# Four key heads per load on 32 partitions each, with block transposes of the weights, in a cached-attention decode kernel

## The chip, the cores and the metric

The kernel runs on one core of one Trainium2 chip. The metric is the device time of one execution in microseconds (us).

## The reference, cut to what matters

For 8 batch rows with one token each, the reference computes a gated sum of an attention over a key/value cache and a small MLP.

```python
W = min(4096, max(256, Sk // 4))          # 1024: only the last 1024 of 4096 cached keys count
q = (x @ wq)                              # 16 query heads of 256, 2 for each of 8 key heads
k = jnp.repeat(k_cache[:, :, Sk - W:, :], rep, axis=1)
v = jnp.repeat(v_cache[:, :, Sk - W:, :], rep, axis=1)
p = softmax(einsum("bhqd,bhkd->bhqk", q, k) * Dh ** -0.5)
a = einsum("bhqk,bhkd->bhqd", p, v) ... @ wo
b = gelu(layernorm(x) @ w1 + b1) @ w2 + b2
return g * a + (1 - g) * b                # g = sigmoid(sum(x * gate_w))
```

All data is bf16. The keys and values that count are 8 x 8 x 1024 x 256 elements each, 67.1 MB together. The four weight matrices add 10.5 MB. Each key and value byte is used for two query heads only, so there is little arithmetic for each byte.

With these inputs the attention adds only a very small part to the output: with the values set to zero, the reference's output of rms 0.025 changes by an rms of 0.00004. The comparison with the reference therefore passes even when keys and values lie in the wrong order.

## The kernel before: the parts that matter

The work goes in 16 units. A unit is one batch row and four key heads, 2 MB of keys and 2 MB of values. Each 1 MB load holds two heads, interleaved over the partitions, and each partition receives one run of 8 KB:

```python
def kv_loader(src, b, g):                      # GP = 2 heads, NCK = 16 keys in a run
    def load(t):
        nc.sync.dma_start(
            t[:],                              # 128 partitions: p = 2 * s + head
            src[b, g : g + GP, kv_base:Sk, :].rearrange("a (s c) d -> s a (c d)", c=NCK),
        )
```

The loads go to a ring of 18 slots of 1 MB. The compute of a unit turns the keys on TensorE (PE), copies them out on VectorE (DVE) and ScalarE (ACT), makes the scores, and turns the exponentials with 16 small matmuls. The values are the stationary operand:

```python
def values(u, ET, rb):
    ...
            for j in range(NJ):
                for c in range(NCK):
                    o = c * Dh + j
                    nc.tensor.matmul(PO[:, j, cols],
                        lhsT=vn[:, o : (c + 1) * Dh : NJ],       # 128 x 128 values as weights
                        rhs=ET[:, c, cols], start=(c == 0), stop=(c == NCK - 1))
...
for u in range(1, NQ - 2):
    transpose_keys(u)
    values(u - 1, *weights(u - 1))
    scores(u)
    softmax(u)
```

Of the kernel before, what the change touches and what calls it, by code (L numbers as in the profile page):

```python
# [17 lines left out]
def kernel(  # L18
# [38 lines left out]
    GP = 2  # L57
    NCK = NC * GP
    SK = P // GP
    SLOT = 4096  # L60
# [4 lines left out]
    RING = 18  # L65
    NMM = 512
    CMM = NMM // SK
# [30 lines left out]
    def kv_loader(src, b, g):  # L98
        def load(t):
            nc.sync.dma_start(  # L100
                t[:],
                src[b, g : g + GP, kv_base:Sk, :].rearrange(
                    "a (s c) d -> s a (c d)", c=NCK
                ),
            )

        return load
# [22 lines left out]
    def add_kv(name, src, u):  # L130
        b, half = divmod(u, Hkv // QUAD)
        for s in range(2):
            add((name, u, s), kv_loader(src, b, half * QUAD + 2 * s))

    wq_m = A_wq[0:DM, :].rearrange("(p r) n -> p r n", r=NR)
# [5 lines left out]
    W2A = SLOT // D  # L141

    add_kv("k", A_k_cache, 0)
    add(("w1", 0), rows_loader([w1_m[:, 0 : 2 * F]]))
    add(("w1", 1), rows_loader([w1_m[:, 2 * F : 3 * F], w1_t]))
    for r in range(NR):
        add(("wq", r), rows_loader([wq_m[:, r, :]]))
    add(("wq", NR), rows_loader([wq_t]))
    add(("w2", 0), rows_loader([w2_v[:, 0 : W2A * D]]))
    add(("w2", 1), rows_loader([w2_v[:, W2A * D : NF * D]]))  # L150
# [7 lines left out]
    for q in range(NHQ):  # L158
        for j0, j1 in WO_PARTS[q]:
            add(("wo", q, j0), rows_loader([wo_v[:, q, j0 * D : j1 * D]]))  # L160

    def slot(*key):
        return slots[index[key]]
# [19 lines left out]
    nc.vector.memset(S_ps[:], 0.0)  # L183

# [15 lines left out]
    sel = consts.tile([P, RQ], BF16)  # L200
    qw = consts.tile([P, NJ, NB, Hq], BF16)
# [18 lines left out]
    for h in range(2):  # L220
        nc.vector.tensor_copy(xz[:, h, h::2], x_sb[:, DM:D])
    transposed(xT, x_sb, xz)
    nc.vector.tensor_copy(
        sel[:].rearrange("p (a i) -> p a i", i=rep),
        ident[:].rearrange("p (a s) -> p a s", a=QUAD)[:, :, 0:rep],
    )

    par = consts.tile([P, GP], F32)
    own = consts.tile([P, RQ], F32)
    nc.vector.reduce_sum(  # L230
        par[:], ident[:].rearrange("p (s a) -> p a s", a=GP), axis=AXIS.X
    )
    nc.vector.tensor_copy(
        own[:].rearrange("p (t a i) -> p t a i", a=GP, i=rep),
        par[:]
        .rearrange("p (t a i) -> p t a i", t=1, i=1)
        .to_broadcast([P, QUAD // GP, GP, rep]),
    )
# [61 lines left out]
    def transpose_keys(u):  # L300
        for s in range(2):
            kn = slot("k", u, s)
            kt = ktpool.tile([P, NJ, NCK, SK, GP], BF16, tag="kt", name="kt")
            KT[s] = kt
            ktf = kt[:].rearrange("p j c s a -> p j (c s a)")
            for c0 in range(0, NCK, NC):
                for j in range(NJ):
                    ktp = ps_kt.tile([P, W], BF16, tag="ktp", name="ktp")
                    for c in range(NC):
                        o = (c0 + c) * Dh + j * P  # L310
                        nc.tensor.transpose(  # L311
                            ktp[:, c * P : (c + 1) * P], kn[:, o : o + P], ident[:]
                        )
                    dst = ktf[:, j, c0 * P : (c0 + NC) * P]
                    if evac[0] % 8 in (2, 4, 7):
                        nc.scalar.copy(dst, ktp[:])  # L316
                    else:
                        nc.vector.tensor_copy(dst, ktp[:])  # L318
                    evac[0] += 1
            done()  # L320

    def query():
        qt = ps_misc.tile([P, Hq * NJ, NB], F32, tag="misc", name="qt")
        for r in range(NR + 1):
            w = slot("wq", r)
            for k in range(Hq * NJ):
# [4 lines left out]
                    lhsT=w[:, c : c + P],  # L331
# [5 lines left out]
            done()  # L337
        for j in range(NJ):
            nc.vector.tensor_scalar_mul(  # L339
                qw[:, j, :, :],  # L340
                qt[:].rearrange("p (h j) b -> p j b h", j=NJ)[:, j],
                qscale,
            )

    def scores(u):
        b, half = divmod(u, Hkv // QUAD)
        for hf in range(W // NMM):
            for j in range(NJ):
                for a in range(QUAD):
                    h0 = (half * QUAD + a) * rep  # L350
                    nc.tensor.matmul(  # L351
                        S_ps[32 * a : 32 * a + rep, hf * NMM : (hf + 1) * NMM],
                        lhsT=qw[:, j, b, h0 : h0 + rep],
                        rhs=KT[a // GP][:, j, hf * CMM : (hf + 1) * CMM, :, a % GP],
# [6 lines left out]
    def softmax(u):  # L361
        nmx = epool.tile([P, 1], F32, tag="nmx", name="nmx")
        nc.vector.reduce_max(nmx[:], S_ps[:], axis=AXIS.X, negate=True)  # L363
        E = epool.tile([P, W * GP], BF16, tag="E", name="E")
        rowsum = epool.tile([P, 1], F32, tag="rowsum", name="rowsum")
        nc.scalar.activation(  # L366
            E[:].rearrange("p (k a) -> p k a", a=GP),
            S_ps[:].rearrange("p (k o) -> p k o", o=1).to_broadcast([P, W, GP]),
            ACT.Exp,
            bias=nmx[:],  # L370
            scale=1.0,
            accum_out=rowsum[:],
# [3 lines left out]
    def weights(u):  # L376
        E, rowsum = soft.pop(u)
        rsum = epool.tile([P, 1], F32, tag="rsum", name="rsum")
        nc.vector.reciprocal(rsum[:], rowsum[:])
        selr = epool.tile([P, RQ], F32, tag="selr", name="selr")  # L380
        nc.vector.tensor_scalar(  # L381
            selr[:], sel[:], rsum[:], float(GP), op0=ALU.mult, op1=ALU.mult
        )
        sm = ps_sm.tile([P, NCK + 1, RQ], F32, tag="sm", name="sm")
# [208 lines left out]
```

## Time and profile before

| | before |
|---|---|
| time, median of 3 runs | 198.85 us (198.73 to 199.01) |
| span of the profiled run | 197.0 us |
| DMA queue of SyncE, share of 16 engines' span | 95.8% |
| rate in the middle of the run | 406 to 427 GB/s |
| one 8 KB packet (trace's DMA records, mean) | 317 ns |
| one 4 KB packet | 162 ns |
| loop of one unit in the chain of waits | 10.15 us |

From the two packet sizes, 4,096 B more cost 155 ns, which is 26.4 GB/s for one of the 16 DMA engines, and about 7 ns per packet are left over. Sixteen engines at 26.4 GB/s would make 422 GB/s.

The page of the kernel before: the busy tenths of the DMA engines and the rate in 40 equal slices of the span, and the queue that carries the loads.

```profile
DMA  4999999999999999999999999999999999999960
GB/s 170 416 427 406 420 412 414 421 414 424 411 414 419 419 419 416 414 419 419 423 411 411 423 416 423 409 418 423 416 416 413 418 419 419 421 411 416 413 246 23
...
q1 hardware_dynamic: 11424, 77.68, 95.8%
```

The DMA engines are busy to 9 tenths or more in every slice from the second to the 38th, at an even rate. This stream is the first limit. The costliest groups of compute come next, as line, engine, operation, output and inputs, then busy time and mean time of one instruction, then the idle time before them:

```profile
L311 PE MATMUL ktp<-ident,slot 128*128 128x128 bf16 x1024 | 73.9, 232 | 21.6 <-ACT kt L316 15.2
...
L366 ACT ACTIVATE E<-S_ps,nmx 128x2048 bf16<-128x2048 f32 x16 | 31.5, 1968 | 72.2 <-DVE nmx L363 72.2
...
L414 PE MATMUL po<-ET,slot 128*128 128x4 bf16 x1024 | 28.1, 164 | 5.3 <-DVE ET L395 5.3
...
L351 PE MATMUL S_ps<-kt,qw 128*2 128x512 bf16 x256 | 18.1, 402 | 0.4 <-DVE qw L339 0.4
```

The end of the chain of waits, in order of time (start, duration, what):

```profile
118.22 19.89 DMA slot<-in_A_v_cache_dram
...
138.17 21.37 DMA slot<-in_A_v_cache_dram
...
159.60 19.96 DMA slot<-in_A_v_cache_dram
...
179.62 13.82 DMA slot<-in_A_wo_dram
...
193.48 0.39 PE A_ps L545 x6
...
193.89 0.34 DVE res L552
```

From 118 us to 193.4 us the chain consists of loads alone, each one released by the load eight places ahead of it. Before 118 us it runs through compute, in a loop of 10.15 us for a unit. So compute keeps up with the stream, but has almost no slack. With the DMA engines busy throughout, a faster compute alone should gain little here.

### The profile page before, as it was taken

To read this page: it belongs to the slowest core of one execution; us is meant where nothing else is said; L and a number is where in the kernel's file an instruction comes from. 1 tells how busy PE (TensorE), PEld (TensorE's weight loads), DVE (VectorE), ACT (ScalarE), POOL (GpSimd) and SP (SyncE) were. 2 spreads that over 40 slices of the span, in tenths; PEclk is the share of its full clock that TensorE was granted. 3 is DMA by queue.
4 is the path that set the end of the run, shared out by engine and by line. 5 is a ranking of instruction groups with operands and counts; after the bars stand their busy time and mean duration, and the time that the engine had idled before them with its cause. 6 is when DMAs were issued, how large, how long until landed. Compare 5 with 4: busy or idle time off the path is not lost.

```text
span 197.0 us, 6578 instructions
## 1 busy us (share of the span) xinstructions
PE 147.7 (75%) x3006; PEld 125.1 (64%) x3006; DVE 94.3 (48%) x230; ACT 82.0 (42%) x85; POOL 0.9 (0%) x7
## 2 busy tenths in 40 slices
PE   1699869868686878979596868686868686887662
PEld 0699739656574758877575667575656665675641
DVE  6540335364646464555545454636363636763200
ACT  3250043272636354362718180808172727383000
POOL 1000000000000000000000000000000000000000
PEclk9996556999999996799999999999999999997555
DMA  4999999999999999999999999999999999999960
GB/s 170 416 427 406 420 412 414 421 414 424 411 414 419 419 419 416 414 419 419 423 411 411 423 416 423 409 418 423 416 416 413 418 419 419 421 411 416 413 246 23
DMA packets 11645, 78.10 MB, mean 396 GB/s; under 512 B 1489, under 2 KB 1890, under 8 KB 3042
## 3 DMA queue, kind: packets, MB, share of 16 engines
q1 hardware_dynamic: 11424, 77.68, 95.8%
q8 instruction: 23, 0.38, 0.8%
q10 hardware_dynamic: 194, 0.02, 0.1%
q14 instruction: 4, 0.03, 0.0%
HBM read 77.68 MB, written 0.01 MB: 394 GB/s over the span
## 4 chain that ended last, share of the span: by engine, by line
DMA 49%; PE 26%; DVE 16%; ACT 5%; issue 2%; SPq 0%; ACTq 0%
DMA slot<-in_A_v_cache_dram 31%; PE ktp L311 10%; DMA slot<-in_A_wq_dram 8%; DVE kt L318 7%; PE po L414 7%; DMA slot<-in_A_wo_dram 7%; DVE nmx L363 6%; PE S_ps L351 5%; ACT kt L316 4%; DMA slot<-in_A_k_cache_dram 3%; PE sm L393 2%; ACT E L366 1%; DVE ET L395 1%; DVE selr L381 1%; PE bb L484 1%
## 5 line engine op out<-in xcount | busy, mean ns | idle before, releaser
L311 PE MATMUL ktp<-ident,slot 128*128 128x128 bf16 x1024 | 73.9, 232 | 21.6 <-ACT kt L316 15.2
L311 PEld LDWEIGHTS <-slot 128*128 128x128 bf16 x1024 | 66.1, 105 | 33.3 <-issue 28.3
L318 DVE COPY kt<-ktp 128x1024 bf16<-128x1024 bf16 x80 | 52.5, 686 | 30.3 <-PE ktp L311 29.0
L366 ACT ACTIVATE E<-S_ps,nmx 128x2048 bf16<-128x2048 f32 x16 | 31.5, 1968 | 72.2 <-DVE nmx L363 72.2
L316 ACT COPY kt<-ktp 128x1024 bf16<-128x1024 bf16 x48 | 47.1, 1013 | 19.3 <-PE ktp L311 19.3
L414 PEld LDWEIGHTS <-slot 128*128 128x128 bf16 x1024 | 29.5, 99 | 6.8 <-issue 6.8
L414 PE MATMUL po<-ET,slot 128*128 128x4 bf16 x1024 | 28.1, 164 | 5.3 <-DVE ET L395 5.3
L363 DVE TENSOR_REDUCE nmx<-S_ps 128x1 f32<-128x1024 f32 x16 | 19.6, 1225 | 13.0 <-PE S_ps L351 13.0
L351 PE MATMUL S_ps<-kt,qw 128*2 128x512 bf16 x256 | 18.1, 402 | 0.4 <-DVE qw L339 0.4
L423 DVE TENSOR_TENSOR oT<-po,rb 128x8 bf16<-128x8 f32 x32 | 4.3, 190 | 26.5 <-PE po L414 26.5
L393 PE MATMUL sm<-selr,ones_f 128*128 128x8 f32 x32 | 6.6, 279 | 5.5 <-DVE selr L381 5.5
L386 PE MATMUL sm<-sel,E 128*128 128x8 bf16 x256 | 8.8, 167 | 1.7 <-ACT E L366 1.7
L393 PEld LDWEIGHTS sm<-selr,ones_f 128*128 128x128 f32 x32 | 5.2, 203 | 6.8 <-DVE selr L381 6.6
L386 PEld LDWEIGHTS <-E 128*128 128x128 bf16 x256 | 8.2, 97 | 1.8 <-ACT E L366 1.8
L395 DVE TENSOR_TENSOR ET<-sm,own 128x128 bf16<-128x128 f32 x16 | 4.7, 291 | 8.2 <-PE sm L393 8.2
L351 PEld LDWEIGHTS <-qw 128*2 128x2 bf16 x256 | 4.7, 82 | 5.2 <-DVE qw L339 0.5
L545 PE MATMUL A_ps<-slot,oP 128*8 128x112 bf16 x128 | 4.3, 290 | 2.8 <-DMA slot<-in_A_wo_dram 2.1
L545 PEld LDWEIGHTS <-oP 128*8 128x8 bf16 x128 | 2.9, 113 | 4.1 <-issue 3.4
L329 PE MATMUL qt<-xT,slot 128*128 128x8 bf16 x128 | 3.9, 168 | 0.8 <-DMA slot<-in_A_wq_dram 0.4
L329 PEld LDWEIGHTS <-slot 128*128 128x128 bf16 x128 | 3.7, 104 | 1.0 <-DMA slot<-in_A_wq_dram 0.6
L381 DVE TENSOR_SCALAR selr<-sel,rsum 128x8 f32<-128x8 bf16 x16 | 3.7, 231 | 0.6
L552 DVE SCALAR_TENSOR_TENSOR res<-A_ps,gg_s,mixb 128x112 bf16<-128x112 f32 x1 | 0.3, 335 | 6.6 <-PE A_ps L545 6.6
(69 smaller groups left out, 38.9 us busy)
## 6 DMA issues: line engine op xcount, KB each, us to landing
slot<-in_A_k_cache_dram SPq DMA_DIRECT2D x32, 1024.0 KB, 19.9
slot<-in_A_v_cache_dram SPq DMA_DIRECT2D x32, 1024.0 KB, 19.9
slot<-in_A_wq_dram SPq DMA_DIRECT2D x3, 1024.0 KB
slot<-in_A_wo_dram SPq DMA_DIRECT2D x3, 896.0 KB, 19.1
slot<-in_B_w_dram SPq DMA_DIRECT2D x1, 1008.0 KB
slot<-in_B_w_dram SPq DMA_DIRECT2D x1, 896.0 KB
slot<-in_B_w_dram SPq DMA_DIRECT2D x1, 560.0 KB
slot<-in_A_wq_dram SPq DMA_DIRECT2D x1, 512.0 KB
```

What stands on the lines that cost most here:

```text
L311: nc.tensor.transpose(ktp[:, c * P : (c + 1) * P], kn[:, o : o + P], ident[:])
L316: nc.scalar.copy(dst, ktp[:])
L318: nc.vector.tensor_copy(dst, ktp[:])
L329: nc.tensor.matmul(qt[:, k, :], lhsT=w[:, c : c + P], rhs=xT[:, r + half, :], start=(r == 0 and k == 0), stop=(r == NR), skip_group_check= ...
L351: nc.tensor.matmul(S_ps[32 * a : 32 * a + rep, hf * NMM : (hf + 1) * NMM], lhsT=qw[:, j, b, h0 : h0 + rep], rhs=KT[a // GP][:, j, hf * CMM ...
L363: nc.vector.reduce_max(nmx[:], S_ps[:], axis=AXIS.X, negate=True)
L366: nc.scalar.activation(E[:].rearrange("p (k a) -> p k a", a=GP), S_ps[:].rearrange("p (k o) -> p k o", o=1).to_broadcast([P, W, GP]), ACT.Exp,
L386: nc.tensor.matmul(sm[:, c, :], lhsT=E[:, c * P : (c + 1) * P], rhs=sel[:], start=True, stop=True,)
L393: nc.tensor.matmul(sm[:, NCK, :], lhsT=ones_f[:], rhs=selr[:], start=True, stop=True)
L395: nc.vector.tensor_tensor(ET[:], sm[:, 0:NCK, :], own[:].rearrange("p (o r) -> p o r", o=1).to_broadcast([P, NCK, RQ]), op=ALU.mult,)
L414: nc.tensor.matmul(PO[:, j, cols], lhsT=vn[:, o : (c + 1) * Dh : NJ], rhs=ET[:, c, cols], start=(c == 0), stop=(c == NCK - 1),)
L545: nc.tensor.matmul(dst, lhsT=oP[:, j, q, :], rhs=w[:, o + cols.start : o + cols.stop], start=(q == 0 and j == 0), stop=(q == NHQ - 1 and j ...
```

## The change

The intent was to load all four heads of a unit at once, in runs of 16 KB, and to lay each head on its own 32 partitions. Then the exponentials can be turned in 32x32 blocks on VectorE, and the values can be the moving operand of matmuls placed in four column tiles of PE. The diff, cut to its core (setup of constants, weights' slots and index changes left out):

```diff
-    GP = 2
-    NCK = NC * GP
-    SK = P // GP
-    SLOT = 4096
-    RING = 18
+    SK = P // QUAD          # 32 partitions for each of QUAD = 4 heads
+    NCK = W // SK           # 32 keys in a run: 16 KB
+    SLOT = 8192
+    RING = 9
...
-            nc.sync.dma_start(
-                t[:],
-                src[b, g : g + GP, kv_base:Sk, :].rearrange(
-                    "a (s c) d -> s a (c d)", c=NCK
-                ),
-            )
+            n = NCK * Dh // parts
+            for i in range(parts):
+                for a in range(QUAD):
+                    nc.sync.dma_start(
+                        t[a * SK : (a + 1) * SK, i * n : (i + 1) * n],
+                        v[a, :, i * n : (i + 1) * n],
+                    )
...
 def softmax(u):
+        nc.vector.tensor_tensor(nmx[:], nmx[:], cap[:], op=ALU.min)
-        E = epool.tile([P, W * GP], BF16, tag="E", name="E")
+        E = epool.tile([P, W], BF16, tag="E", name="E")
...
 def weights(u):
-        for c in range(NCK):
-            nc.tensor.matmul(sm[:, c, :], lhsT=E[:, c * P : (c + 1) * P], rhs=sel[:], ...)
+        nc.vector.transpose(ET[:].rearrange("p c r -> p (c r)"), E[:])
...
 def values(u, ET, rsel):
+        for c in range(NCK):
+            t = c % QUAD
+            nc.tensor.matmul(
+                PO[32 * t : 32 * t + RQ, :],
+                lhsT=ET[:, c, 0:RQ],
+                rhs=vn[:, c * Dh : (c + 1) * Dh], ...)
+        nc.vector.tensor_copy(os_[:], PO[:])
+        for j in range(NJ):
+            nc.tensor.matmul(sm[:, j, :], lhsT=os_[:, j::NJ], rhs=rsel[:], start=True, stop=True)
```

The bytes moved stay the same. What was one load of 1 MB on 128 partitions is now two loads of 512 KB, each on 32 neighbouring partitions, one after the other on the same queue.

More of the change, by code (lines that the diff above doesn't have):

```diff
@@ L56 @@
     NQ = NB * Hkv // QUAD
-    GP = 2
-    NCK = NC * GP
-    SK = P // GP
-    SLOT = 4096
+    SK = P // QUAD
+    NCK = W // SK
+    NH = 2
+    CH = NCK // NH
+    SLOT = 8192
     HPQ = 4
@@ L64 @@
     WO_PARTS = [[(0, NJ8)]] * (NHQ - 1) + [[(0, 4), (4, 6), (6, 8)]]
-    RING = 18
-    NMM = 512
-    CMM = NMM // SK
+    RING = 9
+    BIG = 1e30
     qscale = float(Dh) ** -0.5
@@ L96, in done, with kv_loader @@
         pump()
-    def kv_loader(src, b, g):
-        def load(t):
-            nc.sync.dma_start(
-                t[:],
-                src[b, g : g + GP, kv_base:Sk, :].rearrange(
-                    "a (s c) d -> s a (c d)", c=NCK
-                ),
-            )
+    def kv_loader(src, u, parts):
+        b, half = divmod(u, Hkv // QUAD)
+        v = src[b, half * QUAD : (half + 1) * QUAD, kv_base:Sk, :].rearrange(
+            "a (s c) d -> a s (c d)", c=NCK
+        )
+        def load(t):
+            n = NCK * Dh // parts
[4 more added lines that the diff above has]
+                        v[a, :, i * n : (i + 1) * n],
+                    )
         return load
@@ L128, in add, with add_kv @@
         plan.append(loader)
-    def add_kv(name, src, u):
-        b, half = divmod(u, Hkv // QUAD)
-        for s in range(2):
-            add((name, u, s), kv_loader(src, b, half * QUAD + 2 * s))
-    wq_m = A_wq[0:DM, :].rearrange("(p r) n -> p r n", r=NR)
+    def add_kv(name, src, u, parts=1):
+        add((name, u), kv_loader(src, u, parts))
+    wq_m = A_wq[0:DM, :].rearrange("(p r) n -> p (r n)", r=NR)
     wq_t = A_wq[DM:D, :].rearrange("r (h n) -> (r h) n", h=2)
@@ L140 @@
     wo_v = A_wo.rearrange("(q p j) n -> p q (j n)", p=P, j=NJ8)
-    W2A = SLOT // D
-    add_kv("k", A_k_cache, 0)
-    add(("w1", 0), rows_loader([w1_m[:, 0 : 2 * F]]))
-    add(("w1", 1), rows_loader([w1_m[:, 2 * F : 3 * F], w1_t]))
-    for r in range(NR):
-        add(("wq", r), rows_loader([wq_m[:, r, :]]))
-    add(("wq", NR), rows_loader([wq_t]))
-    add(("w2", 0), rows_loader([w2_v[:, 0 : W2A * D]]))
-    add(("w2", 1), rows_loader([w2_v[:, W2A * D : NF * D]]))
+    add_kv("k", A_k_cache, 0, parts=2)
+    add(("w1",), rows_loader([w1_m, w1_t]))
+    add(("wq", 0), rows_loader([wq_m[:, 0 : 2 * HD]]))
+    add(("wq", 1), rows_loader([wq_m[:, 2 * HD : 3 * HD], wq_t]))
+    add(("w2",), rows_loader([w2_v]))
     for u in range(1, NQ - 1):
@@ L157 @@
         add_kv("v", A_v_cache, u)
-    for q in range(NHQ):
-        for j0, j1 in WO_PARTS[q]:
-            add(("wo", q, j0), rows_loader([wo_v[:, q, j0 * D : j1 * D]]))
+    for q in range(0, NHQ, 2):
+        add(
+            ("wo", q),
+            rows_loader(
+                [
+                    wo_v[:, q + i, j0 * D : j1 * D]
+                    for i in range(2)
+                    for j0, j1 in WO_PARTS[q + i]
+                ]
+            ),
+        )
     def slot(*key):
@@ L183 @@
     nc.vector.memset(S_ps[:], 0.0)
+    PO = ps_po.tile([P, Dh], F32)
+    nc.vector.memset(PO[:], 0.0)
     NX = NR + 2
@@ L199 @@
     yT = consts.tile([P, NX, NB], BF16)
-    sel = consts.tile([P, RQ], BF16)
-    qw = consts.tile([P, NJ, NB, Hq], BF16)
+    sel = consts.tile([P, RQ], F32)
+    qw = consts.tile([P, NJ, NB, Hq // RQ, QUAD, RQ], BF16)
     oT = consts.tile([P, Hq, NJ, NB], BF16)
@@ L222 @@
     transposed(xT, x_sb, xz)
-    nc.vector.tensor_copy(
-        sel[:].rearrange("p (a i) -> p a i", i=rep),
-        ident[:].rearrange("p (a s) -> p a s", a=QUAD)[:, :, 0:rep],
-    )
-    par = consts.tile([P, GP], F32)
-    own = consts.tile([P, RQ], F32)
-    nc.vector.reduce_sum(
-        par[:], ident[:].rearrange("p (s a) -> p a s", a=GP), axis=AXIS.X
-    )
-    nc.vector.tensor_copy(
-        own[:].rearrange("p (t a i) -> p t a i", a=GP, i=rep),
-        par[:]
-        .rearrange("p (t a i) -> p t a i", t=1, i=1)
-        .to_broadcast([P, QUAD // GP, GP, rep]),
-    )
+    nc.vector.reduce_sum(
+        sel[:], ident[:].rearrange("p (a s) -> p s a", a=QUAD)[:, 0:RQ, :], axis=AXIS.X
+    )
+    cap = consts.tile([P, 1], F32)
+    rows = consts.tile([P, 1], F32)
+    for a in range(QUAD):
+        nc.vector.reduce_sum(
+            rows[32 * a : 32 * a + 32, :],
+            ident[32 * a : 32 * a + 32, (32 + rep) * a : (32 + rep) * a + rep],
+            axis=AXIS.X,
+        )
+    nc.vector.tensor_scalar(
+        cap[:], rows[:], 2.0 * BIG, -BIG, op0=ALU.mult, op1=ALU.add
+    )
+    nc.vector.memset(qw[:], 0.0)
     def norm_and_gate():
@@ L300, in transpose_keys @@
     def transpose_keys(u):
-        for s in range(2):
-            kn = slot("k", u, s)
-            kt = ktpool.tile([P, NJ, NCK, SK, GP], BF16, tag="kt", name="kt")
-            KT[s] = kt
-            ktf = kt[:].rearrange("p j c s a -> p j (c s a)")
-            for c0 in range(0, NCK, NC):
+        kn = slot("k", u)
+        for hf in range(NH):
+            kt = ktpool.tile([P, NJ, CH, P], BF16, tag="kt", name="kt")
+            KT[hf] = kt
+            for c0 in range(0, CH, NC):
                 for j in range(NJ):
-                    ktp = ps_kt.tile([P, W], BF16, tag="ktp", name="ktp")
+                    ktp = ps_kt.tile([P, NC, P], BF16, tag="ktp", name="ktp")
                     for c in range(NC):
-                        o = (c0 + c) * Dh + j * P
-                        nc.tensor.transpose(
-                            ktp[:, c * P : (c + 1) * P], kn[:, o : o + P], ident[:]
-                        )
-                    dst = ktf[:, j, c0 * P : (c0 + NC) * P]
+                        o = (hf * CH + c0 + c) * Dh + j * P
+                        nc.tensor.transpose(ktp[:, c, :], kn[:, o : o + P], ident[:])
+                    dst = kt[:, j, c0 : c0 + NC, :]
                     if evac[0] % 8 in (2, 4, 7):
@@ L319, in transpose_keys @@
                     evac[0] += 1
-            done()
+        done()
     def query():
@@ L324, in query @@
         for r in range(NR + 1):
-            w = slot("wq", r)
+            w, o = slot("wq", r // 2), (r % 2) * HD
             for k in range(Hq * NJ):
@@ L330, in query @@
                     qt[:, k, :],
-                    lhsT=w[:, c : c + P],
+                    lhsT=w[:, o + c : o + c + P],
                     rhs=xT[:, r + half, :],
@@ L336, in query @@
                 )
-            done()
-        for j in range(NJ):
-            nc.vector.tensor_scalar_mul(
-                qw[:, j, :, :],
-                qt[:].rearrange("p (h j) b -> p j b h", j=NJ)[:, j],
-                qscale,
-            )
+        done(2)
+        qv = qt[:].rearrange("p (g a i j) b -> p a j b g i", g=Hq // RQ, a=QUAD, i=rep)
+        for a in range(QUAD):
+            for j in range(NJ):
+                nc.vector.tensor_scalar_mul(
+                    qw[:, j, :, :, a, a * rep : (a + 1) * rep], qv[:, a, j], qscale
+                )
     def scores(u):
         b, half = divmod(u, Hkv // QUAD)
-        for hf in range(W // NMM):
+        for hf in range(NH):
             for j in range(NJ):
                 for a in range(QUAD):
-                    h0 = (half * QUAD + a) * rep
                     nc.tensor.matmul(
-                        S_ps[32 * a : 32 * a + rep, hf * NMM : (hf + 1) * NMM],
-                        lhsT=qw[:, j, b, h0 : h0 + rep],
-                        rhs=KT[a // GP][:, j, hf * CMM : (hf + 1) * CMM, :, a % GP],
+                        S_ps[32 * a : 32 * a + RQ, hf * CH * SK : (hf + 1) * CH * SK],
+                        lhsT=qw[:, j, b, half, a, :],
+                        rhs=KT[hf][:, j, :, a * SK : (a + 1) * SK],
                         start=(j == 0),
@@ L363, in softmax @@
         nc.vector.reduce_max(nmx[:], S_ps[:], axis=AXIS.X, negate=True)
-        E = epool.tile([P, W * GP], BF16, tag="E", name="E")
+        nc.vector.tensor_tensor(nmx[:], nmx[:], cap[:], op=ALU.min)
+        E = epool.tile([P, W], BF16, tag="E", name="E")
         rowsum = epool.tile([P, 1], F32, tag="rowsum", name="rowsum")
         nc.scalar.activation(
-            E[:].rearrange("p (k a) -> p k a", a=GP),
-            S_ps[:].rearrange("p (k o) -> p k o", o=1).to_broadcast([P, W, GP]),
-            ACT.Exp,
-            bias=nmx[:],
-            scale=1.0,
-            accum_out=rowsum[:],
+            E[:], S_ps[:], ACT.Exp, bias=nmx[:], scale=1.0, accum_out=rowsum[:]
         )
@@ L377, in weights @@
         E, rowsum = soft.pop(u)
-        rsum = epool.tile([P, 1], F32, tag="rsum", name="rsum")
-        nc.vector.reciprocal(rsum[:], rowsum[:])
         selr = epool.tile([P, RQ], F32, tag="selr", name="selr")
-        nc.vector.tensor_scalar(
-            selr[:], sel[:], rsum[:], float(GP), op0=ALU.mult, op1=ALU.mult
-        )
-        sm = ps_sm.tile([P, NCK + 1, RQ], F32, tag="sm", name="sm")
-        for c in range(NCK):
-            nc.tensor.matmul(
-                sm[:, c, :],
-                lhsT=E[:, c * P : (c + 1) * P],
-                rhs=sel[:],
-                start=True,
-                stop=True,
-            )
@@ L393, in weights @@
-        nc.tensor.matmul(sm[:, NCK, :], lhsT=ones_f[:], rhs=selr[:], start=True, stop=True)
-        ET = epool.tile([P, NCK, RQ], BF16, tag="ET", name="ET")
-        nc.vector.tensor_tensor(
-            ET[:],
-            sm[:, 0:NCK, :],
-            own[:].rearrange("p (o r) -> p o r", o=1).to_broadcast([P, NCK, RQ]),
-            op=ALU.mult,
-        )
-        rb = epool.tile([P, RQ], F32, tag="rb", name="rb")
-        nc.vector.tensor_copy(rb[:], sm[:, NCK, :])
-        return ET, rb
-    def values(u, ET, rb):
-        b, half = divmod(u, Hkv // QUAD)
-        PO = ps_po.tile([P, NJ, RQ], F32, tag="po", name="po")
-        for s in range(2):
-            vn = slot("v", u, s)
-            cols = slice(GP * rep * s, GP * rep * (s + 1))
-            for j in range(NJ):
-                for c in range(NCK):
-                    o = c * Dh + j
-                    nc.tensor.matmul(
-                        PO[:, j, cols],
-                        lhsT=vn[:, o : (c + 1) * Dh : NJ],
-                        rhs=ET[:, c, cols],
-                        start=(c == 0),
-                        stop=(c == NCK - 1),
-                    )
-            done()
-        for j in range(NJ):
-            nc.vector.tensor_tensor(
-                oT[:, half * RQ : (half + 1) * RQ, j, b],
-                PO[:, j, :],
-                rb[:],
-                op=ALU.mult,
-            )
@@ new lines, in weights @@
+        nc.vector.tensor_scalar_mul(selr[:], sel[:], rowsum[:])
+        sm = ps_sm.tile([P, RQ], F32, tag="sm", name="sm")
+        nc.tensor.matmul(sm[:], lhsT=ones_f[:], rhs=selr[:], start=True, stop=True)
+        ET = epool.tile([P, NCK, 32], BF16, tag="ET", name="ET")
+        nc.vector.transpose(ET[:].rearrange("p c r -> p (c r)"), E[:])
+        rb = epool.tile([P, RQ], F32, tag="rb", name="rb")
+        nc.vector.reciprocal(rb[:], sm[:])
+        rsel = epool.tile([P, RQ], F32, tag="rsel", name="rsel")
@@ new lines, in weights, with values @@
+        nc.vector.tensor_tensor(rsel[:], rb[:], sel[:], op=ALU.mult)
+        return ET, rsel
+    def values(u, ET, rsel):
+        b, half = divmod(u, Hkv // QUAD)
+        vn = slot("v", u)
+        for c in range(NCK):
[3 more added lines that the diff above has]
+                lhsT=ET[:, c, 0:RQ],
+                rhs=vn[:, c * Dh : (c + 1) * Dh],
+                start=(c < QUAD),
+                stop=(c >= NCK - QUAD),
+            )
+        done()
+        os_ = epool.tile([P, Dh], F32, tag="os", name="os_")
+        nc.vector.tensor_copy(os_[:], PO[:])
+        sm = ps_sm.tile([P, NJ, RQ], F32, tag="sm", name="sm")
+        for j in range(NJ):
+            nc.tensor.matmul(
+                sm[:, j, :], lhsT=os_[:, j::NJ], rhs=rsel[:], start=True, stop=True
+            )
+        nc.vector.tensor_copy(
+            oT[:, half * RQ : (half + 1) * RQ, :, b].rearrange("p h j -> p j h"), sm[:]
+        )
@@ L430, in mlp_hidden @@
     def mlp_hidden():
         hT = ps_misc.tile([P, NF, NB], F32, tag="misc", name="hT")
-        w1a, w1b = slot("w1", 0), slot("w1", 1)
+        w = slot("w1")
         for r in range(NR):
-            w, o = (w1a, r * F) if r < 2 else (w1b, 0)
+            o = r * F
             for c in range(NF):
@@ L447, in mlp_hidden @@
                     hT[64 * h : 64 * h + 64, c, :],
-                    lhsT=w1b[:, F + c : F + FH : NF],
+                    lhsT=w[:, NR * F + c : NR * F + FH : NF],
                     rhs=yT[:, NR + h, :],
@@ L453, in mlp_hidden @@
                 )
-        done(2)
+        done()
         z = consts.tile([P, NF, NB], F32)
@@ L481, in mlp_out @@
         for c in range(NF):
-            w, o = (slot("w2", 0), c) if c < W2A else (slot("w2", 1), c - W2A)
+            w = slot("w2")
             for dst, cols in quads(bb):
@@ L486, in mlp_out @@
                     lhsT=hs[:, c, :],
-                    rhs=w[:, o * D + cols.start : o * D + cols.stop],
+                    rhs=w[:, c * D + cols.start : c * D + cols.stop],
                     start=(c == 0),
@@ L494, in mlp_out @@
             )
-        done(2)
+        done()
         nc.vector.tensor_scalar_mul(mixb[:], bb[:], gg_s[:, 1:2])
@@ L539 @@
     for q in range(NHQ):
-        for j0, j1 in WO_PARTS[q]:
-            w = slot("wo", q, j0)
-            for j in range(j0, j1):
-                for dst, cols in quads(A_ps):
-                    o = (j - j0) * D
-                    nc.tensor.matmul(
-                        dst,
-                        lhsT=oP[:, j, q, :],
-                        rhs=w[:, o + cols.start : o + cols.stop],
-                        start=(q == 0 and j == 0),
-                        stop=(q == NHQ - 1 and j == NJ8 - 1),
-                    )
+        w = slot("wo", q - q % 2)
+        for j in range(NJ8):
+            o = ((q % 2) * NJ8 + j) * D
+            for dst, cols in quads(A_ps):
+                nc.tensor.matmul(
+                    dst,
+                    lhsT=oP[:, j, q, :],
+                    rhs=w[:, o + cols.start : o + cols.stop],
+                    start=(q == 0 and j == 0),
+                    stop=(q == NHQ - 1 and j == NJ8 - 1),
+                )
     nc.vector.scalar_tensor_tensor(
```

## The prediction

> **What bounds the kernel now.** The DMA stream. The slice table shows DMA at 9 tenths from slice 2 to 37, at 406 to 427 GB/s; the queue table puts 95.8% of the 16 engines' span on the SyncE queue. Key and value loads are 64 transfers of 1 MB, 67.1 of 77.7 MB. The 8 KB packets took 317 ns, 4 KB ones 162 ns: 4,096 B more cost 155 ns, 26.4 GB/s per engine, plus about 7 ns per packet. Compute is close behind: the chain of waits repeats every 10.15 us per unit of 4 MB, but it is DMA from 118 us on, and the last load lands at 193.4 of 197.0 us.
>
> **What the change removes.** On PE: 1,024 value matmuls and weight loads (28.1 and 29.5 us) become 512 moving 256 columns in four column tiles, estimated at 1.05 us per unit from the scores' 16 x 512 columns in 1.03 us; 256 turning matmuls (8.8 us) go. On ACT the exponential halves, 1.97 to about 1.1 us. **Adds.** On DVE per unit one 32x32-block transpose of 128x1024 (estimate 1.1 to 1.2 us, like the 1.22 us reduce[...]), a 256-column fp32 copy (0.35), four small ops (0.15 to 0.2 each); on PE two fp32 matmuls for the output (0.4 us). DVE goes from about 5.9 to 7 us per unit, PE falls to about 7.3. The serial loop stays at 9.5 to 10.5 us. If the stream kept its rate, 16 KB packets save about 7 ns in 634, 1% or 1 to 2 us, minus twice as many completion writes (9 ns each): 197 to 198.
>
> **What it moves: the stream.** Each 1 MB transfer on 128 partitions becomes two of 512 KB on 32 partitions. [...] This trace has no such load to agree or disagree. The order of instructions puts all four heads on one queue, at most eight transfers in flight by eight rotating completion semaphores. [...] 67.1 MB in 318 us, other loads 25 us, start and tail 5 us: about 348 us. [...]
>
> **Prediction.** 305 us, range 196 to 355: faster by over 2% 0.04, within 2% 0.25, slower by over 2% 0.71. All of the loss is on the critical path.
>
> **What would show it.** Key and value packets of 16 KB at about 1.2 us rather than 0.63; DMA still at 9 tenths while GB/s in the slices falls to 210 to 290; weight slices (before about 22 us) still at about 410; PE and DVE waiting for key and value loads; SyncE waiting for earlier transfers' landings; the chain nearly all DMA. Right on compute: exponential 1.1 us, transpose 1.1 to 1.2, values 1.05 per unit, PE busy near 105 us.
>
> **What would make it wrong.** [...] then 16 KB packets take about 0.63 us and the result is within 2%. Or the new DVE to PE round trips push the loop above 10.15 us, which costs 2 to 6 us.

The sum put the keys and values at 211 GB/s, half of the 422 worked out above: 318 us for 67.1 MB, and 348 us with the other terms. Also cut are the sums for a rate that recovers in part, 220 to 320 us, and for one that doesn't fall, 197 us. The point of 305 lies between them.

## The result, and the profile after

The changed kernel takes 349.62 us (median of 4 runs, 348.81 to 351.8), against 198.93 us for the kernel before in the same rounds. The ratio is 1.7594, with a 95% interval of 1.7504 to 1.7683. Ratios here are the mean time of one kernel's fast runs over that of the other's fast runs of the same rounds, so they are not quite the ratio of the medians that are quoted.

The same lines of the page of the changed kernel:

```profile
DMA  8999999999999999999999999999999999999991
GB/s 175 342 407 285 208 213 211 211 211 211 211 211 211 213 213 213 214 212 224 221 211 214 222 220 216 213 224 218 216 216 224 220 216 218 224 216 222 222 344 64
...
q1 hardware_dynamic: 8112, 77.68, 98.1%
```

The DMA engines are as busy as before, 98.1% of their time, but the rate is halved: 208 to 224 GB/s in slices 5 to 38. Slice 3 stands out with 407 GB/s. There the weights are loaded, whose transfers still land on all 128 partitions. So the engines did not become slower in general, and the loss belongs to the key and value loads. In the trace's DMA records a 16 KB packet takes 1,201 ns on average, while the two packets of 8 KB that carried as much before took 634 ns.

The compute groups that answer to those of before:

```profile
L319 PE MATMUL ktp<-ident,slot 128*128 128x128 bf16 x1024 | 93.9, 276 | 75.6 <-DMA slot<-in_A_k_cache_dram 72.6
...
L396 PE MATMUL PO<-slot,ET 128*8 128x256 bf16 x512 | 26.9, 379 | 50.1 <-issue 33.7
L372 ACT ACTIVATE E<-S_ps,nmx 128x1024 bf16<-128x1024 f32 x16 | 17.8, 1113 | 140.9 <-DVE nmx L369 140.9
...
L384 DVE STREAM_TRANSPOSE ET<-E 128x1024 bf16<-128x1024 bf16 x16 | 19.8, 1237 | 0.0
```

The exponential fell from 1,968 to 1,113 ns, and the block transpose costs 1,237 ns. PE shows more busy time than before for the key transposes, not less, because it was granted a lower clock: the mean is 0.636 of full speed, against 0.896 before. The run wide16k below has the same matmuls at a mean clock of 0.938, and there one takes 227 ns and not 276. PE idles between loads, as two of its waits show (engine, line, what it waited for: total, times, longest):

```profile
PE ktp L319 <- DMA slot<-in_A_k_cache_dram: 72.6, 15, 8.3
...
PE PO L396 <- DMA slot<-in_A_v_cache_dram: 16.4, 4, 4.9
```

Some links of the chain of waits in order of time:

```profile
37.40 19.87 DMA slot<-in_A_k_cache_dram
...
57.29 19.86 DMA slot<-in_A_k_cache_dram
...
292.13 19.03 DMA slot<-in_A_v_cache_dram
...
311.18 18.95 DMA slot<-in_A_v_cache_dram
...
330.14 14.85 DMA slot<-in_A_wo_dram
...
345.02 0.39 PE A_ps L528 x6
```

The chain is nothing but loads from 37 us to the last one at 345 us. Each link is eight transfers long, 8 x 512 KB = 4.19 MB. In 19.87 us that is 211 GB/s, half of the 422 worked out above. Late in the run, 18.95 us for the same bytes are 221 GB/s. So the stream became slightly faster as it ran, and the cause of that is one of the questions below.

### The profile page after: what moved, and what is told of

Its sections match the earlier page's. It is cut to its first block, busy times and chain, and to the rows that moved or that the text cites. A ratio compares the mean times of both kernels' runs of the same rounds, so it can differ in the third digit from the quotient of the medians.

```text
span 348.5 us, 5296 instructions
## 1 busy us (share of the span) xinstructions
PE 189.4 (54%) x2302; PEld 145.8 (42%) x2302; DVE 120.8 (35%) x257; ACT 71.1 (20%) x85; POOL 0.8 (0%) x7
## 3 DMA queue, kind: packets, MB, share of 16 engines
q1 hardware_dynamic: 8112, 77.68, 98.1%
## 4 chain that ended last, share of the span: by engine, by line
DMA 98%; ACTq 0%; issue 0%; PE 0%; DVE 0%; SPq 0%
DMA slot<-in_A_k_cache_dram 82%; DMA slot<-in_A_v_cache_dram 11%; DMA slot<-in_A_wo_dram 4%; DMA b_r<-in_B_b_dram 1%; ACTq L179 0%; PE A_ps L528 0%; DVE res L535 0%; SPq L108 0%
## 5 line engine op out<-in xcount | busy, mean ns | idle before, releaser
L319 PE MATMUL ktp<-ident,slot 128*128 128x128 bf16 x1024 | 93.9, 276 | 75.6 <-DMA slot<-in_A_k_cache_dram 72.6
L319 PEld LDWEIGHTS <-slot 128*128 128x128 bf16 x1024 | 89.7, 130 | 89.8 <-issue 89.4
L396 PE MATMUL PO<-slot,ET 128*8 128x256 bf16 x512 | 26.9, 379 | 50.1 <-issue 33.7
L372 ACT ACTIVATE E<-S_ps,nmx 128x1024 bf16<-128x1024 f32 x16 | 17.8, 1113 | 140.9 <-DVE nmx L369 140.9
L396 PEld LDWEIGHTS <-ET 128*8 128x8 bf16 x512 | 14.8, 109 | 57.1 <-issue 46.9
L356 PE MATMUL S_ps<-kt,qw 128*8 128x512 bf16 x256 | 29.8, 606 | 0.3 <-DVE qw L347 0.3
L384 DVE STREAM_TRANSPOSE ET<-E 128x1024 bf16<-128x1024 bf16 x16 | 19.8, 1237 | 0.0
L356 PEld LDWEIGHTS <-qw 128*8 128x8 bf16 x256 | 6.7, 104 | 9.4 <-issue 7.9
L411 DVE CAST oT<-sm 128x16 bf16<-128x16 f32 x16 | 3.6, 228 | 17.8 <-PE sm L408 17.8
L335 PEld LDWEIGHTS <-slot 128*128 128x128 bf16 x128 | 3.6, 104 | 2.5 <-DMA slot<-in_A_wq_dram 2.5
L380 DVE TENSOR_SCALAR selr<-sel,rowsum 128x8 f32<-128x8 f32 x16 | 3.5, 218 | 0.0
```

The costliest lines, as they stand in the source:

```text
L319: nc.tensor.transpose(ktp[:, c, :], kn[:, o : o + P], ident[:])
L335: nc.tensor.matmul(qt[:, k, :], lhsT=w[:, o + c : o + c + P], rhs=xT[:, r + half, :], start=(r == 0 and k == 0), stop=(r == NR), skip_grou ...
L356: nc.tensor.matmul(S_ps[32 * a : 32 * a + RQ, hf * CH * SK : (hf + 1) * CH * SK], lhsT=qw[:, j, b, half, a, :], rhs=KT[hf][:, j, :, a * SK ...
L372: nc.scalar.activation(E[:], S_ps[:], ACT.Exp, bias=nmx[:], scale=1.0, accum_out=rowsum[:])
L384: nc.vector.transpose(ET[:].rearrange("p c r -> p (c r)"), E[:])
L396: nc.tensor.matmul(PO[32 * t : 32 * t + RQ, :], lhsT=ET[:, c, 0:RQ], rhs=vn[:, c * Dh : (c + 1) * Dh], start=(c < QUAD), stop=(c >= NCK - ...
```

## The experiments

The theory, called the landing theory: in this stream, what halves the rate is that a transfer lands on a group of neighbouring partitions and is not spread over the 128. The rates so far agree, 208 to 224 GB/s against 406 to 427 before.

Four rivals could also explain a halved rate: runs of 16 KB may be slow in themselves; the new DVE and PE steps may hold the buffers; transfers of 512 KB may be too small or too many; and the reads of one head at a time may collide in the memory.

### wide16k: the same runs of 16 KB on all partitions

```diff
-            "a (s c) d -> a s (c d)", c=NCK
+            "a (s c) d -> s a (c d)", c=NCK
...
-                for a in range(QUAD):
-                    nc.sync.dma_start(t[a * SK : (a + 1) * SK, ...], v[a, :, ...])
+                nc.sync.dma_start(t[:, i * n : (i + 1) * n], v[:, :, i * n : (i + 1) * n])
```

> The changed kernel's compute, but each 2 MB key or value block is one transfer on 128 partitions, four heads interleaved, still in 16 KB runs (wrong result on purpose: the layout no longer fits the compute). [...] 16 KB packets fall from 1.20 to about 0.63 us, slices at 415 to 422 GB/s, 196 to 199 us. Rival 1 (16 KB runs are slow in themselves): 16 KB packets stay near 1.2 us and the time near 350 us. Rival 2 (the new DVE and PE round trips hold the buffers): DMA is no longer at 9 tenths and the time stays over 210 us.

Measured: 198.31 us, ratio 1.0011 to before (0.9942 to 1.0079), 16 KB packets at 618 ns. The slices of its page:

```profile
GB/s 164 424 439 396 435 425 419 424 428 424 428 421 428 421 428 428 424 428 424 428 419 428 424 424 428 424 426 421 428 424 428 428 424 428 421 422 406 373 93 3
```

The whole loss is gone, with all of the new compute in place (the keys are in the wrong order for it, but the instructions are the same). The first two rivals fall: runs of 16 KB are fast, and the new steps don't hold the stream below the speed of before. The mid-run rate, mostly 419 to 428 GB/s, is even about 2% above that of before.

That this faster stream gains no time is told by the loop. Two units by their windows (stretch: length; busy time of each engine; granted clock, DMA share, GB/s):

```profile
62.43:72.61 10.18, 7.21 (x121) 5.55 (x119) 6.76 (x14) 4.03 (x5) 0.00 (x0) 1.00 1.00 423
72.61:82.79 10.18, 7.21 (x121) 5.55 (x120) 6.76 (x14) 4.03 (x5) 0.00 (x0) 1.00 1.01 425
```

A unit takes 10.18 us of compute, at full clock. At 426 GB/s its 4.19 MB need only 9.85 us. So compute limits this version, and the loop of 10.18 us is a new wait that takes the place of the old one.

### wide_onehead: one head for each transfer, on all partitions

```diff
-            "a (s c) d -> a s (c d)", c=NCK
+            "a (s c) d -> a s (c d)", s=P
...
+            n = NC * Dh
+            for a in range(QUAD):
+                nc.sync.dma_start(t[:, a * n : (a + 1) * n], v[a])
```

> The changed kernel's compute, four transfers of 512 KB for each block, one head each, read from the same 512 KB of memory as in the changed kernel, but landing on all 128 partitions in 4 KB runs (wrong result on purpose). [...] 4 KB packets at 0.162 us, per transfer and engine 8 x 0.162 plus 0.01 = 1.31 us, so 128 transfers take 167 us, and about 201 to 204 us in all. Rival 3 (512 KB transfers, twice as many, only 4 MB in flight) and rival 4 (all engines read one head's region at once): about 211 to 224 GB/s and 340 to 350 us.

Measured: 202.15 us, ratio 1.0162 (1.0147 to 1.0177), with 4 KB packets at 164 ns. The slices of its page:

```profile
GB/s 201 412 443 392 423 404 403 409 406 411 405 410 409 408 410 406 409 407 408 405 410 409 406 410 405 406 410 405 411 406 410 405 410 406 411 405 415 417 220 9
```

Apart from the first key block, the number and the size of the transfers are those of the changed kernel, and each one reads the same 512 KB of one head. Neither costs anything beyond the packets' overhead, which the expectation had added up. The third rival falls, and the fourth in its simple form.

### narrow8k: each head's load in two, with runs of 8 KB

```diff
-    def add_kv(name, src, u, parts=1):
+    def add_kv(name, src, u, parts=2):
```

> The changed kernel with each head on its 32 partitions in two transfers of 8 KB runs instead of one of 16 KB. [...] packets of 8 KB at about 0.60 us instead of the 0.317 us of before, GB/s 211 to 224, 345 to 355 us. Rival 1 (run length): packets at 0.32 us and about 199 us.

Measured: 305.26 us in one run (state unknown), 8 KB packets at 522 ns on average. The run length is not what makes the loads slow, as packets of half the size are still far from 317 ns. But the time missed the expectation of 345 to 355 us by 40 us, and the slices show how:

```profile
GB/s 167 282 416 382 219 219 220 224 225 225 231 231 237 244 242 250 245 247 252 251 261 271 267 274 272 266 271 269 269 272 277 277 281 284 269 255 252 253 379 61
```

The key and value stream starts at 219 GB/s and climbs to 284. The landing theory doesn't say why it climbs. In slices 36 to 38 the rate falls back to about 253, and no run explains that.

### before64: the kernel before, with one head on 64 partitions

```diff
-            nc.sync.dma_start(
-                t[:],
-                src[b, g : g + GP, kv_base:Sk, :].rearrange(
-                    "a (s c) d -> s a (c d)", c=NCK
-                ),
-            )
+            for a in range(GP):
+                nc.sync.dma_start(
+                    t[a * SK : (a + 1) * SK, :],
+                    src[b, g + a, kv_base:Sk, :].rearrange("(s c) d -> s (c d)", c=NCK),
+                )
```

> The kernel before, with each 1 MB load of two heads on 128 interleaved partitions split into two loads of one head on 64 neighbouring partitions (wrong result on purpose: the layout no longer fits). Packets stay 8 KB, compute stays that of before. [...] 8 KB packets near 0.60 us, 211 to 224 GB/s, 340 to 350 us. [...] Rival 2 (the new compute): 199 us.

Measured: 305.36 us in one run (state unknown). The compute here is that of the kernel before, so the new compute has no part in the loss. (A sum gave 199 to 200 us in case 64 partitions cost nothing.)

```profile
GB/s 153 255 421 399 213 218 213 218 214 220 225 222 223 227 234 235 244 241 244 255 272 272 276 291 291 291 288 280 277 270 282 284 270 287 300 277 263 243 343 60
```

The rate begins at 213 GB/s and climbs towards 300. So transfers to 64 neighbouring partitions start at about the same rate as those to 32 (213 against 208 GB/s in slice 5). The climb was again not expected.

### The second theory: phase

The climb suggested a refinement, called the phase theory. It supposes that the rate recovers the sooner, the fewer bytes of the stream land on partitions 0 to 63 before it changes to 64 to 127, or back. These bytes are called the half-period here; they are counted to a boundary at partition 64. In the changed kernel it is two heads of 512 KB, so 1 MB. In narrow8k it is two loads of 256 KB, and in before64 one load of 512 KB, so 512 KB in both.

### order0213: the same transfers in another order

```diff
-                for a in range(QUAD):
+                for a in (0, 2, 1, 3):
```

> The changed kernel with the four head transfers issued in the order 0, 2, 1, 3[...]. [...] GB/s climbs from 211 to 260 or more as in the runs with 8 KB packets, 290 to 325 us. Rival (16 KB packets are what keeps it slow, 8 KB ones what makes it faster): 345 to 352 us as in the changed kernel.

Measured: 306.58 us in one run (state unknown). The packets are still 16 KB, each transfer still goes to the same 32 partitions, and only the half-period fell to 512 KB.

```profile
GB/s 176 299 425 376 211 223 221 221 226 221 228 234 237 232 256 256 241 241 233 241 242 262 262 256 258 262 263 267 271 275 277 299 282 271 301 312 301 223 327 29
```

The stream starts at 211 GB/s as in the changed kernel, but climbs to between 270 and 312. Three kernels with a half-period of 512 KB take 305.3, 305.4 and 306.6 us, although their packets, their compute and their row counts differ. The changed kernel has 1 MB and takes 349.6 us. The phase theory had named 290 to 325 us in advance, so this supports it, and it refutes run length as a cause once more. All of them begin alike, at 208 to 219 GB/s in slice 5. So the half-period doesn't set the rate at which they start, but how far it grows. Why it grows is not shown: no trace here shows single engines.

### low64 and mid64: where the rows of a 64-row transfer land

```diff
-                for a in range(QUAD):
-                    nc.sync.dma_start(t[a * SK : (a + 1) * SK, ...], v[a, :, ...])
+                for p0, a0, a1 in [(0, 0, 2), (64, 2, 3), (96, 3, 4)]:      # low64
+                for p0, a0, a1 in [(0, 0, 1), (32, 1, 3), (96, 3, 4)]:      # mid64
+                    nc.sync.dma_start(
+                        t[p0 : p0 + (a1 - a0) * SK, i * n : (i + 1) * n],
+                        v[a0:a1, :, i * n : (i + 1) * n].rearrange("a s n -> s a n"),
+                    )
```

> The changed kernel with three transfers per 2 MB block, all with 16 KB runs: 64 rows to partitions 0 to 63, 32 rows to 64 to 95, 32 rows to 96 to 127 (wrong layout on purpose). [...] 211 to 225 GB/s and 330 to 352 us. Rivals (size or number of rows or transfers): the same time as mid64, whatever it is, because the two differ only in where the rows land.

> As low64, but the 64 rows land on partitions 32 to 95 and the two 32-row transfers on 0 to 31 and 96 to 127. [...] 1 MB at 422 GB/s (2.48 us) and 1 MB at 211 (4.97 us), so 32 blocks take 238 us, and with 25 us of weights and 5 us of ends about 268 us (255 to 280). Rivals: the same time as low64.

Measured: low64 344.92 us, mid64 338.92 us, one run each (states unknown). The first is as expected. The half-period of low64 is 1 MB, and it falls in with the changed kernel. The second is a miss: 268 us was expected, and the rate in mid64 stays at 190 to 241 GB/s from slice 5 to 38:

```profile
GB/s 174 260 414 336 190 204 216 220 216 212 224 222 233 226 229 231 227 227 235 226 234 236 231 235 231 238 229 237 218 231 231 224 233 231 241 231 233 240 320 27
```

The expectation took the 64-row transfer, which lands on 32 partitions on each side of the boundary, to run at the full 422 GB/s. The run did not bear it out. Why not is not shown: the profile gives no engine number for a packet, and no run here shows which rows an engine takes.

### skew64 and skew_after: an attempt to put the engines out of step

```diff
+            if len(slots) == index[("k", 1)]:            # once, before the second key block
+                nc.sync.dma_start(
+                    delay[:],                            # 8 partitions, never read
+                    A_v_cache[0, 0, 0 : 8 * 8192 // Dh, :].rearrange("(r c) d -> r (c d)", r=8),
+                )
```

In skew64 the base is before64 and the rows are 8 KB. In skew_after the base is the changed kernel and the rows are 16 KB. The extra load was meant to put the DMA engines out of step with each other. That it did is not shown, as the profile names no engines. In each expectation the first range, with its rate, is for the case that this works, and the next is for the case that it has no effect.

> The kernel of before64 (64 rows of 8 KB per head, 305 us, 211 GB/s at first) with one more load before the second key block: 8 rows of 8 KB that nothing reads[...] (the ring has 17 slots instead of 18 to make room). [...] 380 to 420 GB/s at once and 200 to 215 us. [...] 300 to 310 us. A theory without phases (fewer rows or partitions are slow as such): 305 us too, or 1 us more.

> The changed kernel with the same trick: 8 rows of 16 KB onto partitions 0 to 7 [...] before the second key block[...] (8 slots instead of 9). [...] 380 to 425 GB/s at once, 199 to 220 us. [...] 345 to 352 us.

Measured: skew64 302.82 us, where before64 took 305.36; skew_after 336.85 us, where the changed kernel took 349.62 (one run each, states unknown). Neither jumped to full speed: the first slices of keys and values after the delay have 208 and 204 GB/s. In skew_after the rate climbs to 264 late in the run, more than in the changed kernel, and its 336.85 us lie outside both of the ranges that were expected; one run with another ring size cannot tell why.

So the one direct test of what the author held to be behind the phase theory, engines out of step, did not confirm it. The time of skew64 is also close to the 305 us that its expectation gave to a theory without phases. Whether any engine got ahead of another is not shown.

### stride4: only the destination moved

```diff
-                        t[a * SK : (a + 1) * SK, i * n : (i + 1) * n],
+                        t[a::QUAD, i * n : (i + 1) * n],
```

> The changed kernel with only the destination moved: each head's 32 rows of 16 KB go to every fourth partition (a, a+4, ...) instead of 32 neighbours; sources, sizes, number and order of the transfers are the same (wrong layout on purpose). [...] faster than the 307 us of order0213, 199 to 290 us. A rival on the source side (reads of 32 rows of one head collide in the memory): 345 to 352 us.

Measured: 199.65 us in one run (state unknown), 16 KB packets at 618 ns, with 99% of them between 611 and 621 ns.

```profile
GB/s 150 275 408 422 429 421 429 417 424 431 427 417 431 417 427 424 424 422 417 431 422 424 427 424 421 424 419 427 427 424 427 424 427 424 424 424 400 398 136 5
```

This is the cleanest of the runs. Sources, sizes, number, order and queue of the transfers are those of the changed kernel, with 32 rows of 16 KB in each. Only the partitions on which the rows land differ, and the time falls from 349.6 to 199.7 us. The reading side is excluded, and so is the number of rows in a transfer. What is thereby shown is that the place to which the rows are sent decides (the comparison would not notice rows that landed elsewhere). What limits the rate there is not shown by any run.

Slice 2 has 275 GB/s where wide16k has 424, so the first block did suffer. But in the trace's DMA records its packets are not all slow, as most were in the changed kernel: 77% of its 256 packets of 8 KB took at most 330 ns, against 86% in wide16k and 6% in the changed kernel. The block was held up by a few slow packets, 16 of them with over 1 us; why they were slow isn't known.

### wide_reorder and wide_fast: attempts at a version that beats both

wide16k left 10.18 us of compute in a loop whose stream needs 9.85. Two kernels, meant to be right, tried to shorten the loop. Both load as wide16k does, with the heads interleaved, and put the turned weights into that order by a permutation matmul and an ACT copy. Both also move the scores ahead of the values:

```diff
-                        rhs=KT[hf][:, j, :, a * SK : (a + 1) * SK],
+                        rhs=KT[hf][:, j, :, a::QUAD],                 # wide_reorder only
...
+        nc.tensor.matmul(smt[:, 0:NCK, :], lhsT=perm[:], rhs=EB[:, :, 0:RQ], start=True, stop=True)
+        nc.scalar.copy(ET[:], smt[:, 0:NCK, :])
...
         transpose_keys(u)
-        values(u - 1, *weights(u - 1))
         scores(u)
+        Wt = weights(u - 1)
         softmax(u)
+        values(u - 1, *Wt)
...
-                        nc.tensor.transpose(ktp[:, c, :], kn[:, o : o + P], ident[:])
+                        nc.tensor.transpose(ktp[:, c, :], kn[:, o : o + P], permt[:])   # wide_fast only
```

> A right kernel: one 128-partition transfer per block with the four heads interleaved and 16 KB runs; the scores pick a head's keys by a stride of 4; a 128x128 permutation matmul and an ACT copy put the turned weights into the interleaved order; and the scores of a block go ahead of the values of the block before, so that the copy of the value sums and the two fp32 matmuls (0.44 and 0.64 us in wide16k's chain) and the transpose leave the chain. Stream at 424 to 428 GB/s and a loop no longer than 9.9 us: 191 to 195 us, ratio 0.96 to 0.98 to before. If the loop stays near 10.2 us as in wide16k: 197 to 200 us.

> wide_reorder with the key transposes done against a permutation in place of the identity, so that the keys of a head come out next to each other and the scores no longer step by 4 elements. Scores back from 1.98 to about 1.05 us per block, loop from 9.8 to about 8.9 us, under the 9.85 us that the stream needs at 426 GB/s; so the stream ends last again: 191 to 194 us, ratio 0.96 to 0.975. If the loop stays at 9.8: 202 to 204 us.

Measured: wide_reorder 203.68 us, ratio 1.0261 (1.0205 to 1.0317); wide_fast 202.16 us as the median of its three fast runs (200.33 to 202.7; three slow ones took 204.25 to 204.4), ratio 1.0126 (1.0069 to 1.0183) from its fast runs alone. Both miss the gain that was expected. 202 to 204 us had been named for wide_fast in case its loop stayed at 9.8 us, but the loop below did something else. The scores' group of wide_reorder, and then that of wide_fast:

```profile
L357 PE MATMUL S_ps<-kt,qw 128*8 128x512 bf16 x256 | 32.4, 628 | 0.3 <-DVE qw L348 0.3
```

```profile
L363 PE MATMUL S_ps<-kt,qw 128*8 128x512 bf16 x256 | 20.7, 394 | 5.4 <-ACT kt L329 5.1 <-DVE qw L354 0.3
```

With a step of 4 elements in the moving operand a score matmul takes 628 ns, and without it 394 ns. The kernel before steps by 2 and takes 402 ns. The clock is not the reason: in units at a granted clock of 1.00, PE is busy for 2.0 us with the 16 score matmuls at a step of 4, for 1.08 at a step of 2 (before) and for 1.04 without a step (wide16k). wide_fast therefore took the stride away, and its scores were as fast as hoped, but its loop was so only in part. Four units of wide_fast by their windows (this profiled run is a slow one, so its units are compared only with one another):

```profile
61.84:73.64 11.80, 9.93 (x127) 8.53 (x121) 6.96 (x14) 4.61 (x6) 0.00 (x0) 0.71 1.00 423
73.64:83.00 9.36, 7.39 (x127) 5.67 (x123) 6.80 (x15) 4.61 (x6) 0.00 (x0) 1.00 1.00 424
83.00:92.35 9.35, 7.38 (x127) 5.66 (x121) 6.79 (x15) 4.61 (x6) 0.00 (x0) 1.00 1.02 429
92.35:104.26 11.91, 10.04 (x127) 8.63 (x122) 6.97 (x14) 4.61 (x6) 0.00 (x0) 0.71 1.00 423
```

A unit takes 9.35 us at a granted clock of 1.00, under the 9.85 us that the stream needs, and 11.8 to 11.9 us where the clock is 0.71. In the good units PE is busy for 7.38 of 9.35 us (79%), in wide16k for 7.2 of 10.18 us (71%) at a steady 1.00. What lowered the clock is not shown. No run tested whether the denser loop did, and the other traces don't make that simple: wide_onehead, with PE busy for 74% of a good unit (7.35 of 9.97 us), had a mean clock of 0.881 and in two of its units 0.84 and 0.81, and wide_reorder, with 83%, had a mean of 0.891. The fast runs of wide_fast also had a mean clock of only 0.841 to 0.868.

The traces show a second loss. The undisturbed units of wide_reorder took 9.76 to 9.82 us, which is what had been hoped for, in spite of its slow scores. But from the start of the last row maximum to the end of the span it took 19.8 us, and wide16k 15.5. That is 4.3 of the 4.8 us between their spans (200.9 and 196.1). In its chain the values of two units follow that maximum, where wide16k has those of one: the new order had moved them behind it. In wide_fast this end takes 19.7 us. So no version here beats the kernel before. The best of them, wide16k, ties with it, and its layout is wrong for the compute.

## Why the prediction was right, point by point

- **What bounds the kernel: right.** The stream did end last in both kernels, and all of the loss is in the chain as loads.
- **The sum of the halved rate: right.** At 211 GB/s it gave "about 348 us"; 349.62 us and 208 to 224 GB/s were measured. That 348 came so close is partly luck: at the 216 GB/s that the stream had on average from 44 to 331 us, the keys and values take an estimated 311 us and not 318, and so the rest took about 39 us and not 30. The halving was the estimate; the changed kernel and the start of before64 (213 GB/s) bear it out. It is no fixed limit for loads of this form: order0213, with the same destinations, reached 312 GB/s late in its run.
- **The point of 305 us: 45 us low.** The halving came, and what was mis-sized is the chance of a partial recovery, which pulled the point down from 348. The recovery exists, but in the changed kernel, with a half-period of 1 MB, it brought the stream only from 211 to 224 GB/s in 300 us. With the 512 KB of the three other kernels it would have given just that figure, 305 to 307 us. The range of 196 to 355 us was so wide that it held no change as well as a rate halved to the end, and 349.62 lies near its end. That the time fell inside it says little; what the result supports is the sum of the halved rate.
- **What the recovery depends on: supported, not proven.** What the runs show is that order0213 halved the half-period by the order alone and gained 43 us, but the two skew runs did not bring the full rate at will.
- **The signs: right, except for the total of PE (next point).** Packets at "about 1.2 us" were 1.20 us. The weights kept 407 GB/s in their slice. DMA stayed at 9 tenths. PE's wait for keys went to 72.6 us, and SyncE waited 245.7 us in all for earlier key and value loads to land.
- **The compute: mostly right, read from wide16k, where the stream doesn't hide it.** The exponential takes 1.11 us, the transpose 1.24, the values 1.05 to 1.08 per unit, DVE is busy for 6.8 us per unit (predicted 7) and PE for 7.2 (predicted 7.3). The loop of 10.18 us lies in the predicted 9.5 to 10.5. The total of PE "near 105 us" was wrong: 189.4 us in the changed kernel at its low clock, and 136.9 us in wide16k. It did not even agree with the 7.3 us for each of 16 units, which are 117 us already without the projections and the MLP.
- **"If the stream kept its rate": right.** 197 to 198 us were estimated, and wide16k and stride4 took 198.3 and 199.7 us. The prediction gave the gain from the longer packets as 1%; the mid-run rate rose by about 2%, but the compute loop kept it from the total.

## What to carry to other kernels

In this kernel, whose limit is a stream of loads, the partitions that a single transfer lands on mattered more than its size, its run length or the number of transfers: the same loads took 349.6 us on 32 neighbouring partitions and 199.7 us on every fourth one. A busy share does not show this: it was 98.1% at half the rate. Look at the rate in the slices and at the time of one packet. And when a limit is lifted, look at once for the next one: here compute stood 0.3 us per unit behind the stream, so that the faster packets gained nothing.
